# A gated attention/MLP mix on one core: the bias products from GpSimd to VectorE's side work, and a later place for the product with the spread reciprocals

## The chip, the core and the metric

The kernel runs on one core of one Trainium2 chip. The metric is device time in microseconds of one launch. All data are fp32; the large products are made of two or three products of rounded parts (an fp32r part and a remainder), so that each `a @ b` is `ar@br + ar@bl + al@br`.

The engines are named as the profile names them: PE (TensorE, with PEld for its weight loads), DVE (VectorE), ACT (ScalarE), POOL (GpSimd) and SP (SyncE, which here only issues DMAs). POOL issues DMAs as well. Each engine takes its instructions strictly in program order.

## The reference

`x` is 2048 x 512. The output mixes two branches with a gate of each row:

```python
g = sigmoid((x * gate_w).sum(-1, keepdims=True))
q = (x @ wq), 32 heads of 16;  k = x @ wk;  v = x @ wv     # one k and v for all heads
a = softmax(q k^T * 16 ** -0.5) v, heads side by side, @ wo
h = relu(x @ w1 + b1) ** 2                                 # 2048 x 1792
b = h @ w2 + b2
return g * a + (1 - g) * b
```

So `(1 - g) * b2` is one row vector times one number of each row: a 128 x 512 tile of it is one `tensor_scalar` with the broadcast `b2` (`b2t`) and a column of `omg` (1 - g).

## The kernel before

**Attention.** The score matrix is made in units: one unit is 128 keys by 256 queries of four heads. There are 32 groups (4 chunks of 512 rows times 8 groups of four heads) of 32 units each. A unit's scores come out of PE into PSUM (`s`), ACT takes their exponential into `e` (L802), and PE multiplies `e` with the values (`acc`, L825). About two of seven units are relieved: their scores go to a one-bank PSUM tile `x`, DVE copies them to `e` (L786) and ACT takes the exponential there. There is one bank `x`, so a late copy on DVE holds up PE's next score into `x`.

**The rest of the work** is threaded between the scores. PE works on blocks: a block is some units' scores with up to 24 half products ("M") of the other branch between them, then the `acc` products of (mostly) seven units, 56 instructions. What the M's compute comes from a generator of work units: 15 projections of q, then `mlp()`. For each chunk c of 512 rows it yields hidden units (`hidden`, one 128-wide slice f of 1792) in the groups (0..3), (4..7), (8..10), (11..13), and behind each group the four sums of it into `res[c]` (`summed`), which are `res = p * omg + res` on DVE (L700). After chunk c, `res[c]` goes to DRAM (`ress`) by a DMA of POOL (L704); later the output projection reads it back into `big`, adds `g` times its own result and writes `out`. Both of these are POOL DMAs too (L217, L221).

**The bias.** `res[c]` starts as `b2t * omg`: four `tensor_scalar`s of 128 x 512 of POOL at L697, issued when the first group of a chunk is summed. `b2t` is a quarter of a tile called `big`, as is `h[0]`, in which DVE makes the square of relu (L675, L676) before it splits it into `hr` and its remainder (L195, L196). The tile `res` has one buffer (tag `r0`): before the first chunk it belonged to `wqr`, and in each later one it must wait for the DMA of the chunk before.

**The quotients.** When two groups of attention are done, `finish` sends their sums by SP into `oc` (numerators) and `lq` (denominators). `divide` then queues, as DVE work: the bounds and a check of the denominators (L859, L860), the reciprocal `n` (L854) with two POOL DMAs behind it, `ls<-n` (L855) to DRAM and `lc<-ls` (L856) back, which spreads each reciprocal over 16 partitions; and last the product `oc<-oc,lc` (L863), with the DMA `oTs<-oc` of POOL (L897) behind it. There are 15 such quotients.

**What sets the order.** The program's order is made at build time by a planner that keeps a model of the clocks of PE, ACT and DVE. `spend(until)` is called before DVE work that PE waits for and fills DVE's time up to `until` with side work, in this order: remainders of weights that are due, early work (`soon`), `divisions`, `chores` (splitting of loaded tiles into parts). Each entry has a duration and a time from which it may stand; the time of the product `oc<-oc,lc` is the model's end of the copies plus `DIVIDES` (10.0) plus `SPREADS`, so `SPREADS` decides how far behind the reciprocal it stands. None of these figures is a wait on the chip: there every instruction waits for semaphores of what it needs, and those behind it on its engine wait with it.

Of the kernel before, what the change touches and what calls it, by code (L numbers as in the profile page):

```python
# [10 lines left out]
F32 = mybir.dt.float32  # L11
# [4 lines left out]
OP = mybir.AluOpType  # L16
# [16 lines left out]
ROOT = float(0x1fbd1df5 + 0x80000)  # L33
WARM = 10
LW = 4 * CH // 64
LANDS, DIVIDES, WRITES, SPREADS, SURE = 6.0, 10.0, 14.0, 14.0, 1.4
PAIR, CONTEXT, TURN, EXP, COPY, LATE = 0.235, 0.429, 0.36, 0.925, 0.66, 0.3
GROUPS = (0, 1, 2, 3), (4, 5, 6, 7), (8, 9, 10), (11, 12, 13)
AHEAD = 4
# [126 lines left out]
def mix_kernel(ctx: ExitStack, tc: tile.TileContext, xT, wkv, wq, wo, w12, b1, b2, cst, out):  # L166
    nc = tc.nc
# [4 lines left out]
    keep = ctx.enter_context(tc.tile_pool(name="keep", bufs=1))  # L172
# [9 lines left out]
    omg = keep.tile([128, NS], F32, name="omg")  # L182
# [4 lines left out]
    sh = [128, KT, CH]  # L187
# [4 lines left out]
    res = {}  # L192

    def split(r, l, src):
        nc.vector.tensor_copy(r, src)  # L195
        nc.vector.tensor_tensor(l, src, r.bitcast(F32), OP.subtract)  # L196
# [34 lines left out]
    with fast, tc.tile_pool(name="at", bufs=1) as at, \  # L231
# [210 lines left out]
        def stage():  # L442

            if not staged:
                staged.append(keep.tile(sh, F32, name="stage", tag="r2"))
            return staged[0]
# [10 lines left out]
        def dve(d, ready=0.0):  # L457

            nonlocal at_dve
            at_dve = max(at_dve, ready) + d  # L460
            return at_dve
# [30 lines left out]
        def w_rest(half):  # L492
            n = len(ws[half])
            r, l = ws[half][n] = rounded[half][n]
            nc.vector.tensor_tensor(l, wf[half][n], r.bitcast(F32), OP.subtract)
            dve(0.68, since[half][n])
            wanted.append(half)
# [113 lines left out]
        ring, h, b2t, x, osp = [], [], [], dict(enumerate(zip(xr, xl))), {}  # L611

        def later(r, l, src, then=None):

            def cast():
                nc.vector.tensor_copy(r(), src())

            def rest():
                nc.vector.tensor_tensor(l(), src(), r().bitcast(F32), OP.subtract)
                if then:  # L620
                    then()

            chores.extend(((0.46, cast), (0.71, rest)))

        def have(half, n):
            while n not in ws[half]:
                w_split(half)
# [6 lines left out]
        def spend(until=None):  # L634

            nonlocal held

            def fits(d, ready=0.0):
                return until is None or max(at_dve, ready) + d <= until

            while True:
                due = [i for i in halves() if len(rounded[i]) > len(ws[i])]
                if due and fits(0.68, since[due[0]][len(ws[due[0]])]):
                    w_rest(due[0])
                elif soon and fits(soon[0][1]):
                    dve(soon[0][1])
                    soon.pop(0)[2]()
                elif divisions and fits(*divisions[0][:2]):
                    d, ready, f = divisions.pop(0)
                    dve(d, ready)  # L650
                    f()
                elif chores and fits(chores[0][0], held):
                    d, f = chores.pop(0)
                    dve(d, held if d else 0.0)
                    wait = f()
                    if wait:
                        held = max(at_dve, at_pe) + wait
                else:
                    return

        def halves():
            return (0, 1) if len(ws[0]) < begun[0] + 2 else (1, 0)

        def hidden(c, f, hs):

            n = c * NF + f
            have(0, n)
            while c not in x:
                chores.pop(0)[1]()
            (wr, wl), (r, l) = ws[0][n], x[c]  # L670
            begun[0] += 1

            def done(p):
                hr, hl = hs[f] = ring[n % 6]
                nc.vector.tensor_scalar(h[0], p, b1t[:, f:f + 1], 0.0, op0=OP.add, op1=OP.max)  # L675
                nc.vector.tensor_tensor(h[0], h[0], h[0], OP.mult)  # L676
                split(hr, hl, h[0])
                dve(1.9)
                room[0] += 1
                if f == NF - 1 and c < 2:  # L680
                    x_again(c + 2)

            ks = [(k, slice(k * 128, (k + 1) * 128)) for k in range(KT)]
            return ([(wr[:, p], x) for k, p in ks for x in (r[:, k], l[:, k])]
                    + [(wl[:, p], r[:, k]) for k, p in ks], done, None)

        def summed(c, fs, hs):

            n0 = c * NF
            if fs[0] == 0:  # L690
                res[c] = keep.tile(sh, F32, name=f"res{c}", tag="r0")
            have(1, n0 + fs[-1])
            for j in range(4):
                s, cols = 4 * c + j, slice(j * 128, (j + 1) * 128)
                part = res[c][:, j]
                if fs[0] == 0:
                    nc.gpsimd.tensor_scalar(part, b2t[0], omg[:, s:s + 1], None, op0=OP.mult)  # L697

                def done(p, s=s, part=part, j=j):
                    nc.vector.scalar_tensor_tensor(part, p, omg[:, s:s + 1], part, op0=OP.mult, op1=OP.add)  # L700
                    if j == 3:
                        room[1] += len(fs)
                        if fs[-1] == NF - 1:
                            nc.gpsimd.dma_start(ress[c], res[c])  # L704

                yield ([(p[:, cols], ws[1][n0 + f][0]) for f in fs for p in hs[f]]
                       + [(hs[f][0][:, cols], ws[1][n0 + f][1]) for f in fs], done, None)

        def x_again(c):

            r, l = [xp.tile(sh, F32R, name=f"x{n}again{c}", tag=f"x{n}{c - 2}") for n in "rl"]
            def load(a):
                nc.sync.dma_start(stage()[:, :2], xT[c, 2 * a:2 * a + 2].rearrange("k p s -> p k s"))
                return LANDS

            for k in range(KT):
                if k % 2 == 0:
                    chores.append((0.0, lambda k=k: load(k // 2)))
                later(lambda k=k: r[:, k], lambda k=k: l[:, k], lambda k=k: stage()[:, k % 2],
                      (lambda: x.update({c: (r, l)})) if k == KT - 1 else None)  # L720

        def mlp():

            for c in range(NC):
                before, two = None, []
                for fs in GROUPS:
                    hs = {}
                    for f in fs:
                        yield hidden(c, f, hs)
                        o_ready(c)  # L730
                        if c == NC - 1:
                            ask(c, 2)
                        if f == fs[0] and before and fs != GROUPS[-1]:
                            if fs == GROUPS[1] and c > 1:
                                yield from projection(c - 2)
                            yield from summed(*before)
                        elif c > 0 and f > fs[0] and osp.get(c - 1) and c - 1 not in over:
                            yield from projection(c - 1)
                    two = before, (c, fs, hs)
                    before = two[1]  # L740
                for last_two in two:
                    yield from summed(*last_two)
# [227 lines left out]
        def o_ready(c):  # L970

            if c == 0 and not wos:
                wos.extend(xp.tile(sh, F32R, name=n, tag=t) for n, t in (("wor", "xr2"), ("wol", "xl2")))

                def load(a):
                    nc.sync.dma_start(stage()[:, :2], wo[a * 256:a * 256 + 256].rearrange("(t p) n -> p t n", p=128))
                    return WRITES

                for t in range(KT):
                    if t % 2 == 0:  # L980
                        chores.append((0.0, lambda t=t: load(t // 2)))
                    later(lambda t=t: wos[0][:, t], lambda t=t: wos[1][:, t], lambda t=t: stage()[:, t % 2])
            if c > 0:
                ask(c - 1)
# [45 lines left out]
        def projection(c):  # L1030
            if c in over:
                return
            over.add(c)
            yield from wait(c)
            units = list(outproj(c, ots, *osp[c], *wos))
            yield from units[:3]
            terms, done, ahead = units[3]

            def last(p):
                done(p)  # L1040
                used[c] = True

            yield terms, last, ahead
# [258 lines left out]
        for j in range(2, 4):  # L1302
# [3 lines left out]
            s = 4 * (NC - 1) + j  # L1306
# [37 lines left out]
```

## Time and profile before

| what | value |
|---|---|
| median of three runs | 1209.42 us (1207.86 to 1214.25) |
| the profiled execution's own time | 1212.43 us |
| its span, first to last instruction | 1210.7 us |
| mean granted PE clock | 0.995 |
| PE busy | 1190.7 us, 98% of the span |
| ACT busy | 1056.5 us, 87% |
| DVE busy | 744.7 us, 62% |
| POOL busy | 84.4 us, 7% |

A row of the timeline gives start and duration in microseconds, engine, line, operation, output <- input with shapes, and how many instructions were merged (x); in brackets stands the idle time of the engine just before and who ended it. A row of the waits gives the total, the number of times and the longest. A row of the windows gives a stretch, its length, the busy time (and number of instructions) of PE, PEld, DVE, ACT and POOL, then the granted PE clock (1.00 is full), the DMA share and GB/s. A row of the groups ends with the busy time in all and the mean of one in ns, then the idle time before them.

### The profile page before, as it was taken

To read this page: it belongs to the slowest core of one execution; us is meant where nothing else is said; L and a number is where in the kernel's file an instruction comes from. 1 tells how busy PE (TensorE), PEld (TensorE's weight loads), DVE (VectorE), ACT (ScalarE), POOL (GpSimd) and SP (SyncE) were. 2 spreads that over 40 slices of the span, in tenths; PEclk is the share of its full clock that TensorE was granted. 3 is DMA by queue.
4 is the path that set the end of the run, shared out by engine and by line. 5 is a ranking of instruction groups with operands and counts; after the bars stand their busy time and mean duration, and the time that the engine had idled before them with its cause. 6 is when DMAs were issued, how large, how long until landed. Compare 5 with 4: busy or idle time off the path is not lost.

```text
span 1210.7 us, 31619 instructions
## 1 busy us (share of the span) xinstructions
PE 1190.7 (98%) x13685; PEld 789.5 (65%) x13686; DVE 744.7 (62%) x1222; ACT 1056.5 (87%) x1209; POOL 84.4 (7%) x117
## 2 busy tenths in 40 slices
PE   9999899999999999999999999999999999999996
PEld 4566566666666666666666666666666666666663
DVE  6766576666755856657647855657448577556343
ACT  6799799889999889889988988999999899888882
POOL 1001110000000110000002001000001100010000
PEclk9999999999999999999999999999999999999999
DMA  7334432121222222111313123111212222111101
GB/s 230 86 101 116 106 102 64 46 72 55 67 89 93 81 64 97 57 37 44 113 48 115 59 67 106 55 37 54 68 67 64 80 69 92 54 62 40 35 36 38
DMA packets 47656, 89.69 MB, mean 74 GB/s; under 512 B 13642, under 2 KB 14138, under 8 KB 47000
## 3 DMA queue, kind: packets, MB, share of 16 engines
q1 hardware_dynamic: 36664, 64.58, 17.4%
q0 software_dynamic: 10704, 22.77, 5.8%
q8 instruction: 109, 1.79, 0.6%
q14 instruction: 35, 0.29, 0.1%
q10 hardware_dynamic: 144, 0.26, 0.1%
HBM read 61.76 MB, written 21.22 MB: 69 GB/s over the span
## 4 chain that ended last, share of the span: by engine, by line
PE 86%; issue 9%; DVE 2%; DMA 1%; POOL 1%; ACT 0%; SPq 0%; POOLq 0%
PE acc L825 34%; PE mm L1143 29%; PE s L765 17%; PE x L765 4%; POOL qs L358 1%; DMA lc<-ls 1%; DVE e L786 1%; DVE hr L195 0%; DMA xf<-in_xT 0%; PE mm L203 0%; DVE hr L196 0%; PE mm L299 0%; DVE big L676 0%; DVE big L675 0%; PE s L966 0%
## 5 line engine op out<-in xcount | busy, mean ns | idle before, releaser
L802 ACT ACTIVATE e<-s 128x1024 f32<-128x1024 f32 x762 | 748.3, 1029 | 117.4 <-PE s L765 63.7
L786 DVE COPY e<-x 128x512 f32<-128x512 f32 x524 | 361.9, 691 | 406.7 <-PE x L765 334.1
L825 PE MATMUL acc<-e,v_ext 128*32 128x256 f32 (+1 forms) x8064 | 476.2, 385 | 0.0
L765 PE MATMUL s<-qa,k_aug 49*128 49x512 f32 x1524 | 438.2, 416 | 0.1
L825 PEld LDWEIGHTS acc<-e,v_ext 128*32 128x32 f32 x8064 | 247.2, 110 | 198.4 <-issue 55.0
L765 PEld LDWEIGHTS s<-qa,k_aug 49*128 49x128 f32 x1524 | 230.5, 185 | 97.2 <-ACT e L802 73.7
L802 ACT ACTIVATE e<-e 128x1024 f32<-128x1024 f32 x262 | 278.2, 1062 | 3.9 <-DVE e L786 3.9
L765 PE MATMUL x<-qa,k_aug 49*128 49x512 f32 x524 | 218.9, 418 | 9.0 <-DVE e L786 6.8
L1143 PE MATMUL mm<-w2r,hr 64*128 64x512 f32 x752 | 158.2, 394 | 0.0
L765 PEld LDWEIGHTS x<-qa,k_aug 49*128 49x128 f32 x524 | 96.5, 184 | 36.4 <-DVE e L786 13.8
L1143 PEld LDWEIGHTS mm<-w2r,hr 64*128 64x128 f32 x752 | 105.5, 187 | 12.3 <-issue 0.8
L1143 PE MATMUL mm<-w2l,hr 64*128 64x512 f32 x376 | 92.0, 395 | 0.0
L1143 PE MATMUL mm<-xlagain,w1r 64*128 64x512 f32 x224 | 67.3, 392 | 0.0
L1143 PE MATMUL mm<-xragain,w1r 64*128 64x512 f32 x224 | 66.7, 393 | 0.0
L1143 PE MATMUL mm<-xl,w1r 64*128 64x512 f32 x224 | 65.3, 392 | 0.0
L1143 PE MATMUL mm<-xr,w1r 64*128 64x512 f32 x224 | 65.2, 392 | 0.0
L1143 PEld LDWEIGHTS mm<-w2l,hr 64*128 64x128 f32 x376 | 58.9, 188 | 5.8
L1143 PE MATMUL mm<-more 64*128 64x512 f32 x216 | 58.3, 397 | 0.0
L1143 PE MATMUL mm<-xragain,w1l 64*128 64x512 f32 x224 | 51.2, 392 | 0.0
L1143 PE MATMUL mm<-xr,w1l 64*128 64x512 f32 x224 | 50.6, 392 | 0.0
L700 DVE SCALAR_TENSOR_TENSOR res<-mm,omg,res 128x512 f32<-128x512 f32 x64 | 47.5, 741 | 0.0
L855 POOL DMA_DIRECT2D ls<-n x15 | 8.5, 563 | 549.9 <-DVE n L854 494.1
(170 smaller groups left out, 1185.4 us busy)
## 6 DMA issues: line engine op xcount, KB each, us to landing
stage<-in_w SPq DMA_DIRECT2D x56, 256.0 KB
qa<-qs SPq DMA_DIRECT2D x186, 64.0 KB
w1f<-in_w SPq DMA_DIRECT2D x28, 256.0 KB
w2f<-in_w SPq DMA_DIRECT2D x28, 256.0 KB
qs<-qr SPq DMA_DIRECT2D x16, 256.0 KB
ress<-res POOLq DMA_DIRECT2D x4, 1024.0 KB, 4.2
qs<-ql POOLq DMA_DIRECT2D x15, 256.0 KB, 7.7
oc<-accs SPq DMA_DIRECT2D x30, 128.0 KB
```

The lines of the kernel that those rows point to most:

```text
L358: eng.dma_start(bass.AP(tensor=o.tensor, offset=o.offset, ap=[[KS * 2 * CH, 4], [CH, 2 * DH], [1, CH]]), src.bitcast(F32))
L700: nc.vector.scalar_tensor_tensor(part, p, omg[:, s:s + 1], part, op0=OP.mult, op1=OP.add)
L765: nc.tensor.matmul(dst.rearrange("p (a n) -> p a n", a=2), k_aug[rows, kt * 128:(kt + 1) * 128], qa[it][rows, :, q * HC:q * HC + HC], star ...
L786: nc.vector.tensor_copy(e_half(u)[:, 2 * r:2 * r + 2], x.rearrange("p (a n) -> p a n", a=2))
L802: nc.scalar.activation(e_half(u), src, AF.Exp, scale=SCALE)
L825: nc.tensor.matmul(accs[q][h * 32:(h + 1) * 32], v_ext[:, kt], es[u // 2][:, h % 2 * 2 + h // 2, u % 2 * HC:u % 2 * HC + HC * n], start=(k ...
L855: nc.gpsimd.dma_start(ls[i].rearrange("a (b n) -> (a b) n", b=16), n)
L1143: nc.tensor.matmul((self.before if r else self).bank, a[p], b[p], start=not r and i == 0, stop=r == 1 and i == len(self.terms[1]) - 1, ski ...
```

## The change

Two things are changed, and the order on PE stays as it was, row for row.

First, the four bias products of each chunk leave POOL. A list `biases` takes their place: it is filled, and `res[c]` is allocated, once the hidden slice f = 2 of a chunk has been planned, and `spend` takes from it whenever 0.46 us fit, ahead of the chores. They are then `tensor_scalar`s of DVE. If one is still in the list when the first sum needs it, it is issued there.

Second, `SPREADS` goes from 14.0 to 24.0, so that the product `oc<-oc,lc` stands some 10 us further back in DVE's order, and the POOL DMA `oTs<-oc` with it.

```diff
-LANDS, DIVIDES, WRITES, SPREADS, SURE = 6.0, 10.0, 14.0, 14.0, 1.4
+LANDS, DIVIDES, WRITES, SPREADS, SURE = 6.0, 10.0, 14.0, 24.0, 1.4
...
                     d, ready, f = divisions.pop(0)
                     dve(d, ready)
                     f()
+                elif biases and fits(0.46):
+                    bias()
                 elif chores and fits(chores[0][0], held):
...
         def summed(c, fs, hs):
             n0 = c * NF
-            if fs[0] == 0:
-                res[c] = keep.tile(sh, F32, name=f"res{c}", tag="r0")
             have(1, n0 + fs[-1])
             for j in range(4):
                 s, cols = 4 * c + j, slice(j * 128, (j + 1) * 128)
                 part = res[c][:, j]
-                if fs[0] == 0:
-                    nc.gpsimd.tensor_scalar(part, b2t[0], omg[:, s:s + 1], None, op0=OP.mult)
 
                 def done(p, s=s, part=part, j=j):
+                    while (c, j) in biases:
+                        bias()
                     nc.vector.scalar_tensor_tensor(part, p, omg[:, s:s + 1], part, op0=OP.mult, op1=OP.add)
...
+        biases = []
+
+        def bias():
+            c, j = biases.pop(0)
+            s = 4 * c + j
+            dve(0.46)
+            nc.vector.tensor_scalar(res[c][:, j], b2t[0], omg[:, s:s + 1], None, op0=OP.mult)
...
                     for f in fs:
                         yield hidden(c, f, hs)
+                        if f == 2:
+                            res[c] = keep.tile(sh, F32, name=f"res{c}", tag="r0")
+                            biases.extend((c, j) for j in range(4))
                         o_ready(c)
```

**Place 1: DVE while the last projections of q are made** (`qr`, `ql` and `sq` are what DVE makes of one; `e<-x` are the copies of relieved scores). Before, the first product with the spread reciprocals stands two copies behind the split of a projection:

```order
L399 TENSOR_TENSOR sq_143<-qr 128x512
L786 COPY e<-x 128x2x256 x2
L863 TENSOR_TENSOR oc<-oc,lc 128x512
L786 COPY e<-x 128x2x256 x2
L395 CAST qr<-mm 128x512
```

Now (the changed kernel's lines are numbered up to 11 higher):

```order
L399 TENSOR_TENSOR sq_143<-qr 128x512
L797 COPY e<-x 128x2x256 x4
L395 CAST qr<-mm 128x512
L396 TENSOR_TENSOR ql<-mm,qr 128x512
L399 TENSOR_TENSOR sq_143<-qr 128x512
L797 COPY e<-x 128x2x256 x3
L874 TENSOR_TENSOR oc<-oc,lc 128x512
L797 COPY e<-x 128x2x256
L395 CAST qr<-mm 128x512
```

The product has moved past a whole projection and five copies. The other products move in the same way, past some copies each.

**Place 2: DVE behind the split of the second hidden slice of chunk 1** (`orr` and `orl` are the parts of the attention output that the projection will need, `w1l` a remainder of a weight). Before:

```order
L196 TENSOR_TENSOR hr<-big,hr 128x512
L786 COPY e<-x 128x2x256
L619 TENSOR_TENSOR orl<-stage,orr 128x512
L786 COPY e<-x 128x2x256
L495 TENSOR_TENSOR w1l<-w1f,w1r 128x512
L786 COPY e<-x 128x2x256
L616 CAST orr<-stage 128x512
L786 COPY e<-x 128x2x256
L675 TENSOR_SCALAR big<-mm,b1t 128x512
```

Now:

```order
L196 TENSOR_TENSOR hr<-big,hr 128x512
L728 TENSOR_SCALAR res_5002<-big,omg 128x512
L797 COPY e<-x 128x2x256
L495 TENSOR_TENSOR w1l<-w1f,w1r 128x512
L797 COPY e<-x 128x2x256
L728 TENSOR_SCALAR res_5002<-big,omg 128x512
L797 COPY e<-x 128x2x256
L728 TENSOR_SCALAR res_5002<-big,omg 128x512 x2
L797 COPY e<-x 128x2x256
L677 TENSOR_SCALAR big<-mm,b1t 128x512
```

The four bias products take the places of `orl` and `orr`, which move back by one hidden slice, and `w1l` moves ahead by one copy. The other chunks have theirs in the same stretch, chunks 2 and 3 with the fourth behind the next slice.

**Place 3: POOL's queue between two chunks.** Before, the bias products of chunk 1 stand behind the DMA that takes chunk 0 out and between the DMAs of a quotient:

```order
L704 DMA ress<-res_2271 128x2048
L697 TENSOR_SCALAR res_5219<-big,omg 128x512
L855 DMA ls<-n 128x32
L856 DMA lc<-ls 128x1x512
L697 TENSOR_SCALAR res_5219<-big,omg 128x512 x2
L897 DMA oTs<-oc 128x512
L697 TENSOR_SCALAR res_5219<-big,omg 128x512
L217 DMA big<-ress 128x512 x2
```

Now:

```order
L704 DMA ress<-res_2067 128x2048
L866 DMA ls<-n 128x32
L867 DMA lc<-ls 128x1x512
L908 DMA oTs<-oc 128x512
L217 DMA big<-ress 128x512 x2
```

The three rows of bias products are gone, and POOL is left with DMAs alone.

## The prediction

> **What bounds the kernel now.** I read the page's first part, then the timeline of PE for its pace, then the places where that pace breaks, and there DVE and POOL. The first part says which engine has no room:
>
> ```profile
> PE 1190.7 (98%) x13685; PEld 789.5 (65%) x13686; DVE 744.7 (62%) x1222; ACT 1056.5 (87%) x1209; POOL 84.4 (7%) x117
> ```
>
> PE is busy for nearly the whole span, so the change cannot help by making DVE or POOL less busy, only where PE stands still or runs slowly. Since PE's order does not change at all, I compare blocks, from the start of one run of `acc` products to the next. Two ordinary starts, the three around the first break, and what stands on DVE and POOL there:
>
> ```profile
> 172.24 3.23 PE L825 MATMUL acc<-e,v_ext 128*32 128x256 f32 x56
> 180.03 3.23 PE L825 MATMUL acc<-e,v_ext 128*32 128x256 f32 x56
> ...
> 128.48 3.23 PE L825 MATMUL acc<-e,v_ext 128*32 128x256 f32 x56
> 139.84 4.92 PE L825 MATMUL acc<-e,v_ext 128*32 128x256 f32 x56
> 149.29 3.23 PE L825 MATMUL acc<-e,v_ext 128*32 128x256 f32 x56
> ...
> 130.36 0.64 POOL L856 DMA_DIRECT2D lc<-ls  x1 [9.16 <-DMA ls<-n]
> 137.89 0.69 DVE L863 TENSOR_TENSOR oc<-oc,lc 128x512 f32<-128x512 f32 x1 [3.65 <-DMA lc<-ls]
> 139.23 0.49 PE L765 MATMUL x<-qa,k_aug 49*128 49x512 f32 x1 [3.12 <-DVE e L786]
> ```
>
> The pace is 180.03 - 172.24 = 7.79 us. **Break A**: two blocks take 149.29 - 128.48 = 20.81 us. DVE stands 3.65 us at the product with the spread reciprocals, whose DMA was issued at 130.36 and lands at about 137.9; the copy behind it in DVE's queue holds the bank `x`, and PE idles 3.12 us. Then the 56 `acc` products take 4.92 instead of 3.23 us. The windows say why:
>
> ```profile
> 139.80:144.80 5.00, 5.00 (x59) 2.54 (x60) 2.54 (x4) 1.97 (x2) 0.60 (x2) 0.66 0.54 108
> 423.40:427.10 3.70, 3.70 (x18) 2.96 (x20) 2.04 (x4) 1.78 (x2) 0.00 (x0) 0.55 0.00 0
> 172.20:180.00 7.80, 7.80 (x96) 5.26 (x94) 6.88 (x12) 7.00 (x9) 0.53 (x1) 1.00 0.14 31
> ```
>
> Behind A the granted clock is 0.66, in an ordinary block 1.00. The row at 423.40 belongs to **break B**, between chunks 0 and 1; **break C** follows between 1 and 2:
>
> ```profile
> 417.67 1.93 PE L825 MATMUL acc<-e,v_ext 128*32 128x256 f32 x32
> 428.18 3.23 PE L825 MATMUL acc<-e,v_ext 128*32 128x256 f32 x56
> ...
> 706.25 1.93 PE L825 MATMUL acc<-e,v_ext 128*32 128x256 f32 x32
> 712.73 3.23 PE L825 MATMUL acc<-e,v_ext 128*32 128x256 f32 x56
> ...
> 418.80 4.28 POOL L697 TENSOR_SCALAR res<-big,omg 128x512 f32<-128x512 f32 x2
> 419.55 2.11 DVE L195 CAST hr<-big 128x512 fp32r<-128x512 f32 x1
> 423.40 0.53 PE L765 MATMUL x<-qa,k_aug 49*128 49x512 f32 x1 [2.19 <-DVE e L786]
> ...
> 647.44 3.23 PE L825 MATMUL acc<-e,v_ext 128*32 128x256 f32 x56
> 656.75 3.23 PE L825 MATMUL acc<-e,v_ext 128*32 128x256 f32 x56
> ...
> 648.37 6.36 POOL L697 TENSOR_SCALAR res<-big,omg 128x512 f32<-128x512 f32 x4
> 649.65 2.11 DVE L195 CAST hr<-big 128x512 fp32r<-128x512 f32 x1
> 653.51 0.49 PE L765 MATMUL x<-qa,k_aug 49*128 49x512 f32 x1 [1.24 <-DVE e L786]
> ...
> L195 DVE CAST more<-big 128x512 fp32r<-128x512 f32 x9 | 3.8, 427 | 0.3
> ```
>
> The cast of `hr` from `big` takes 2.11 us while POOL's bias products run, against 0.427 us for the same operation elsewhere (last row). The copy behind it is late, PE idles 2.19 us in B and 1.24 in C, and in B the clock falls to 0.55 afterwards. So bias products of an engine that is idle 93% of the time do set PE's end, twice, through DVE.
>
> [...]
>
> **The change part by part.**
>
> *The product, moved back (SPREADS).* A costs 20.81 - 2 x 7.79 = **5.23 us**, 3.6 of standing and 1.7 of slow clock. In place 1 of the order the product now stands five copies and a projection later, just before the copy in the first row below, at about 148.7; less 5.2 us that is 143.5, and the landing at 137.9 does not depend on DVE. So it has 5.6 us to spare, and the gap of 0.67 before that copy takes its 0.69. The 13 other products to which SPREADS applies move by some 10 us too, each with its `oTs` behind it on POOL, which the output projection reads through SP. The other two rows bound that at its tightest, in chunk 3:
>
> ```profile
> 149.40 0.69 DVE L786 COPY e<-x 128x512 f32<-128x512 f32 x1 [0.67 <-PE x L765]
> ...
> 1078.73 0.68 DVE L863 TENSOR_TENSOR oc<-oc,lc 128x512 f32<-128x512 f32 x1
> ...
> 1155.95 0.39 PE L1143 MATMUL mm<-wor,orr 64*128 64x512 f32 x1
> ```
>
> From the product to PE's first use of the parts there are 77 us, of which it takes 10. I take nothing for it, nor for POOL's queue, whose DMAs of this part nobody waits for.
>
> *The bias products off POOL.* B: 10.51 us (428.18 - 417.67) against 6.48 for the block with the same 32 `acc` in front in chunk 2 (712.73 - 706.25): **4.0 us**, 2.2 of standing and 1.8 of slow clock. C: 9.31 - 7.79 = **1.5 us**. The remaining POOL products stretch a DVE instruction here and there without a break in PE's pace: nothing. The gains are 5.2 + 4.0 + 1.5 = 10.7 us.
>
> *The bias products on DVE.* No DVE `tensor_scalar` of 128x512 from SBUF to SBUF stands in the trace. The cast above, also one SBUF tensor in and one out, takes 0.427 us; the same operation with its input in PSUM and a column as scalar takes
>
> ```profile
> L675 DVE TENSOR_SCALAR big<-mm,b1t 128x512 f32<-128x512 f32 x56 | 41.5, 741 | 0.0
> L697 POOL TENSOR_SCALAR res<-big,omg 128x512 f32<-128x512 f32 x16 | 27.4, 1730 | 17.3 <-ACT w1r L500 13.4 <-DMA ress<-res 3.7
> ```
>
> 0.741 us, and POOL needed 1.73. Where the four of a chunk go (place 2), DVE had this room:
>
> ```profile
> 395.66 0.69 DVE L786 COPY e<-x 128x512 f32<-128x512 f32 x1 [0.37 <-PE x L765]
> 396.26 0.68 DVE L619 TENSOR_TENSOR orl<-stage,orr 128x512 fp32r<-128x512 f32 x1
> ...
> 399.06 0.42 DVE L616 CAST orr<-stage 128x512 fp32r<-128x512 f32 x1
> 399.83 0.69 DVE L786 COPY e<-x 128x512 f32<-128x512 f32 x1 [0.35 <-PE x L765]
> ```
>
> That is 0.37 + 0.35 idle, and 0.68 + 0.42 of work that moves back: 1.82 us for 4 x 0.43 = 1.72. The sum fits, the single gaps don't quite: the first product stands in a gap of 0.37, and two stand together. I take 0.1 us a chunk, **0.4** in all. At 0.741 it would be 2.96 - 1.82 = 1.14 a chunk, 4.6 in all, if PE feels each of them; below nothing it cannot go. `orl` and `orr` move back by one slice, a block of 7.8 us; PE reads them only in the projection, a whole group of slices later, and I take nothing for them.
>
> *What DVE now waits for.* POOL used to wait for `b2t` and for `res` to be free, with only DMAs behind it; now DVE would wait, with the copies behind it. For `res` there is time: POOL's product of chunk 1 could start at 382.43, and DVE's first one stands just ahead of the copy at 395.66, 13 us later. For `b2t` there is none to spare:
>
> ```profile
> 141.08 10.17 SPq L358 DMA_DIRECT2D qs<-qr  x2
> ...
> 162.37 0.41 SPq L1059 DMA_DIRECT2D big<-in_b  x1
> ...
> 167.11 0.69 DVE L196 TENSOR_TENSOR hr<-big,hr 128x512 fp32r<-128x512 f32 x1
> ...
> 167.81 4.92 POOL L697 TENSOR_SCALAR res<-big,omg 128x512 f32<-128x512 f32 x3 [13.40 <-ACT w1r L500]
> 168.76 0.42 DVE L616 CAST wor<-stage 128x512 fp32r<-128x512 f32 x1
> ...
> 382.43 1.73 POOL L697 TENSOR_SCALAR res<-big,omg 128x512 f32<-128x512 f32 x1 [3.68 <-DMA ress<-res]
> ```
>
> POOL, idle for 13.4 us, could start at 167.81, just when DVE is done with the split at about 167.75, behind which its first bias product now stands. Both come 5.2 us earlier once A is gone, if SP's chain does: its second `qs<-qr` (the merged row at 141.08 ends at 151.25) is sent when DVE has cast the last `qr`, right behind the copy at 149.40, and from there SP issues on to 162.37. I think that moves along. If `b2` did not come earlier at all, DVE would wait the whole 5.2. Between 0 and 5.2 I take **0.5**, near the row, in which they meet within 0.1.
>
> **The sum**: 10.7 - 0.4 - 0.5 = 9.8 us. Of the profiled execution's 1212.43 us (1.7 of it outside the span) that leaves 1202.6; that execution lies 3.0 above the median of 1209.42, and from the median it is 1199.6. A hangs on when a DMA lands, so part of those 3.0 may be A itself; I take the middle, **1201**.
>
> **The rivals.**
>
> *1. The wait for b2 takes A's place.* For it: the two times meet within 0.1 us, and POOL's DMAs do not all move along and may slow its landing. Against it: SP's issues ahead of 162.37 follow DVE, as said. With the whole 5.2 instead of 0.5, 1205.7.
>
> *2. The product is late again, or the landing moves with it.* The change would not do what it says for A: 1201 + 5.2 = 1206.2. Against it stand 5.6 us to spare.
>
> *3. The long casts do not come from POOL's products.* Then B and C stay, 1201 + 5.5 = 1206.5. For it: the cast at 168.76 took 0.42 in the midst of POOL's products from 167.81. Against it: both casts of 2.11 us lie under such products, and both read `big`, which POOL reads too, while the short one reads `stage`.
>
> *4. Slower: the new product on DVE is as slow as on POOL.* At 1.73 us the four overrun their place by 4 x 1.73 - 1.82 = 5.1 us a chunk, every copy behind them is late by that, and PE waits on the bank `x`: 20.4 in all against 0.4 in the sum, 1201 + 20.0 = 1221. It decides from (10.2 / 4 + 1.82) / 4 = 1.1 us a product. Nothing on DVE of this size and with one input takes that long.
>
> *5. The slow clock is not the stall's doing* and its 1.7 in A and 1.8 in B remain elsewhere: 1204.5. [...] The rows show otherwise: 0.66 and 0.55 right behind 3.12 and 2.19 us of idling, while C, with 1.24, lost only 0.3 beyond that.
>
> **How the numbers follow.** The forecast has 0.72, rival 1 0.09, rivals 2, 3 and 5 0.04 each, rival 4 0.07. The forecast's own range is 1197 (the lowest run, 1207.86, less 10.7) to 1204.5 (the profiled execution less 7.9, with products of 0.741 felt by half). To hold 8 in 10 I take in rivals 1 to 3: 1197 to 1207. A measurement of this kernel can tell about 0.5% from no change, which is 6.0 us: faster means below 1203.4. The forecast lies there in 0.72 x 0.95 = 0.68, the others near 1205 to 1206 in a third of their 0.21: 0.75 in all; the rest of these 0.18; slower, rival 4, 0.07.
>
> **What will show it.** The row of DVE's wait for `lc` is gone and PE has no gap near 134 to 144: part one. No cast of `hr` above 0.5 us, and the blocks that began at 417.67 and 647.44 take about 6.5 and 7.8 us: part two. The 16 new rows of DVE have a mean of 430 ns; above 690 would cost. The first of them, near 162.5, has an idle time in front of it with a DMA as its releaser if rival 1 holds, and PE a gap behind. The prediction is wrong if PE's pace breaks in a new place: first at that one, then at the copies behind the paired bias products.

## The result, and the profile after

The changed kernel takes **1205.87 us** in the median of 20 executions (1200.97 to 1214.08), the kernel before, beside it, 1212.94 (1207.30 to 1220.97). The ratio is 0.9941, 95% interval 0.9922 to 0.9961: faster by 0.4 to 0.8%. The profiled execution took 1207.08 us with a span of 1205.3; that of before had a span of 1210.7. The forecast was 1201, with 1197 to 1207 as its range.

I read the new profile as I read the old one: first the busy times, then PE's pace. The first part of its page:

```profile
PE 1189.2 (99%) x13685; PEld 786.6 (65%) x13686; DVE 745.2 (62%) x1238; ACT 1056.4 (88%) x1209; POOL 56.9 (5%) x101
```

POOL has 16 instructions less and DVE 16 more. DVE's busy time grew by 0.5 us only, though by its groups the products bring 7.3: the casts of `hr` and their remainders take 5.2 us less than before, and the rest is spread over many small differences. The line of the cast, from the views of that line before and after (minimum, median and maximum of one in ns):

```profile
L195 DVE CAST hr<-big x47: 426/427/2114, 158.6 to 1107.9; 128x512 fp32r<-128x512 f32 x47
```

```profile
L195 DVE CAST hr<-big x47: 426/427/429, 153.8 to 1103.5; 128x512 fp32r<-128x512 f32 x47
```

The longest of 47 casts fell from 2.11 to 0.43 us: part two did what it says. Now the timeline of the changed kernel, the starts of PE's blocks around the three old breaks, and DVE's product with the spread reciprocals among them:

```profile
128.73 3.23 PE L836 MATMUL acc<-e,v_ext 128*32 128x256 f32 x56
136.69 3.23 PE L836 MATMUL acc<-e,v_ext 128*32 128x256 f32 x56
143.82 0.68 DVE L874 TENSOR_TENSOR oc<-oc,lc 128x512 f32<-128x512 f32 x1
144.47 3.23 PE L836 MATMUL acc<-e,v_ext 128*32 128x256 f32 x56
...
418.74 1.93 PE L836 MATMUL acc<-e,v_ext 128*32 128x256 f32 x32
425.54 3.23 PE L836 MATMUL acc<-e,v_ext 128*32 128x256 f32 x56
...
644.71 3.23 PE L836 MATMUL acc<-e,v_ext 128*32 128x256 f32 x56
652.49 3.23 PE L836 MATMUL acc<-e,v_ext 128*32 128x256 f32 x56
```

The product has no bracket any more: it waits for nothing. Block against block, before and after:

| place | before, us | after, us | difference |
|---|---|---|---|
| A, two blocks | 20.81 | 15.74 | -5.07 |
| B | 10.51 | 6.80 | -3.71 |
| C | 9.31 | 7.78 | -1.53 |
| the block that begins at 159.56 (164.43 before) | 7.80 | 13.76 | **+5.96** |

The last row is a new break. The timeline of the changed kernel there, with DVE, PE and SP's issue of `b2`:

```profile
159.56 3.23 PE L836 MATMUL acc<-e,v_ext 128*32 128x256 f32 x56
...
162.03 0.42 SPq L1070 DMA_DIRECT2D big<-in_b  x1
162.22 0.69 DVE L196 TENSOR_TENSOR hr<-big,hr 128x512 fp32r<-128x512 f32 x1
...
167.47 0.49 DVE L728 TENSOR_SCALAR res<-big,omg 128x512 f32<-128x512 f32 x1 [4.56 <-DMA big<-in_b]
...
168.61 0.79 PE L776 MATMUL x<-qa,k_aug 49*128 49x512 f32 x1 [4.25 <-DVE e L797]
173.31 3.23 PE L836 MATMUL acc<-e,v_ext 128*32 128x256 f32 x56
```

DVE is through with the split at 162.91 and stands 4.56 us at the first bias product, because `b2` lands at 167.4. The copy behind it frees the bank `x` that much later, and PE idles 4.25 us. The windows of the changed kernel show that its clock suffers afterwards too, while the places of A and B now run at full clock (columns as in the windows of before; the last but two is the granted clock):

```profile
139.80:144.80 5.00, 5.00 (x50) 3.73 (x50) 2.89 (x5) 3.84 (x4) 0.00 (x0) 1.00 0.39 107
...
168.60:173.60 5.00, 4.99 (x34) 3.66 (x38) 3.20 (x7) 1.97 (x2) 0.00 (x0) 0.67 0.15 52
423.40:427.10 3.70, 3.70 (x52) 2.47 (x51) 3.23 (x7) 3.48 (x4) 0.00 (x0) 1.00 0.00 1
```

So of three breaks removed, -10.3 us, this execution gave +6.0 back at a fourth place, 30 us behind the first. That is rival 1.

### The profile page after: what moved, and what is told of

The parts are those of the page before. It is cut to its first block, busy times and chain, and to the rows that moved or that the text cites. A ratio compares the mean times of both kernels' runs of the same rounds, so it can differ in the third digit from the quotient of the medians.

```text
span 1205.3 us, 31610 instructions
## 1 busy us (share of the span) xinstructions
PE 1189.2 (99%) x13685; PEld 786.6 (65%) x13686; DVE 745.2 (62%) x1238; ACT 1056.4 (88%) x1209; POOL 56.9 (5%) x101
## 4 chain that ended last, share of the span: by engine, by line
PE 96%; DVE 2%; DMA 1%; ACT 0%; issue 0%; SPq 0%
PE acc L836 38%; PE mm L1154 32%; PE s L776 19%; PE x L776 5%; DVE e L797 1%; DMA big<-in_b 0%; DMA xf<-in_xT 0%; PE mm L299 0%; PE mm L203 0%; DMA w1f<-in_w 0%; PE s L309 0%; PE s L977 0%; SPq L421 0%; DVE big L678 0%; ACT e L813 0%
## 5 line engine op out<-in xcount | busy, mean ns | idle before, releaser
L677 DVE TENSOR_SCALAR big<-mm,b1t 128x512 f32<-128x512 f32 x56 | 41.6, 743 | 0.0
```

## The experiments

Each kernel was timed beside the kernel before on the same chip; ratios are to that. "After" is the changed kernel.

**1. The later place of the product alone.** The kernel before with one number changed:

```diff
-LANDS, DIVIDES, WRITES, SPREADS, SURE = 6.0, 10.0, 14.0, 14.0, 1.4
+LANDS, DIVIDES, WRITES, SPREADS, SURE = 6.0, 10.0, 14.0, 24.0, 1.4
```

> The kernel before with SPREADS = 24.0 alone; the bias products stay on POOL. Theory (three separate causes): break A near 134 to 149 is gone (20.8 us for two blocks become about 15.7, a gain of 5.1), and DVE waits for no b2, since only POOL does. POOL's products still run, so a cast of hr of 2.1 us with a PE gap of 1.2 to 2.2 us is found again at the two chunk boundaries. What remains of A's gain is cut if ACT, as in the changed kernel, waits 2.2 us for the DMA lq<-accs: by 0 to 2 us. Span about 1206 to 1208, ratio 0.996 to 0.998. Rival (POOL's products have no part in B and C): no cast of hr above 0.5 us at the boundaries, span about 1200 to 1201. Rival (SP's DMAs lag behind whatever DVE does, and the next wait takes all of A back): span about 1210, ratio 1.000.

1206.86 us, ratio 0.9966 (0.9939 to 0.9994). Break A is gone from its trace by the same 5.1 us, and 4.1 of them come back near 160 to 172, where DVE now waits for another late load, with no bias product on it:

```profile
167.46 0.43 DVE L616 CAST wor<-stage 128x512 fp32r<-128x512 f32 x1 [3.25 <-DMA stage<-in_wo]
```

The same kernel has something to say on B and C, because the later products moved POOL's queue. Its timeline, POOL's products and the casts of `hr`:

```profile
418.40 5.82 POOL L697 TENSOR_SCALAR res<-big,omg 128x512 f32<-128x512 f32 x3
419.15 2.11 DVE L195 CAST hr<-big 128x512 fp32r<-128x512 f32 x1
...
423.01 0.50 PE L765 MATMUL x<-qa,k_aug 49*128 49x512 f32 x1 [2.22 <-DVE e L786]
...
647.71 0.43 DVE L195 CAST hr<-big 128x512 fp32r<-128x512 f32 x1
...
659.38 7.28 POOL L697 TENSOR_SCALAR res<-big,omg 128x512 f32<-128x512 f32 x4
```

At C, POOL's four products now start 11.7 us behind the cast, which takes 0.43 us, and the break is gone. At B they stand 0.75 us ahead of it, and it takes 2.11. The long casts go where POOL's products go.

**2. The bias products alone.** After with SPREADS back at 14.0:

```diff
-LANDS, DIVIDES, WRITES, SPREADS, SURE = 6.0, 10.0, 14.0, 24.0, 1.4
+LANDS, DIVIDES, WRITES, SPREADS, SURE = 6.0, 10.0, 14.0, 14.0, 1.4
```

> The changed kernel with SPREADS back at 14.0: the bias products on DVE, the product with the reciprocals where it stood before. Theory (b2 lands at about 167.5 us whether or not A is there): A is back (two blocks take 20 to 21 us), DVE comes to the first bias product at about 167.7 and waits for b2 under 0.5 us, no cast of hr above 0.5 us, B and C are gone: span 1210.7 - 5.3 = about 1205.5, ratio about 0.995. Rival (the wait for b2 comes with the bias products themselves, 4 to 5 us after whatever DVE did before): DVE waits 4 us or more at the first of them, span about 1210 to 1211, ratio about 1.000.

1206.21 us, ratio 0.9966 (0.9939 to 0.9993), but spread from 1200.99 to 1212.64. B and C are gone from its trace. So is break A, although the product stands in its old place:

```profile
128.77 0.64 POOL L867 DMA_DIRECT2D lc<-ls  x1 [7.45 <-DMA ls<-n]
...
134.29 0.68 DVE L874 TENSOR_TENSOR oc<-oc,lc 128x512 f32<-128x512 f32 x1
```

Here the reciprocals were issued at 128.77 and had landed 5.5 us later. In the execution of before they were issued at 130.36 and took 7.5. A is therefore not a fixed property of the order: it depends on how long two transfers take in an execution.

The new break is there in small. SP issues `b2` 1.73 us earlier than in after, DVE is through with the split as early as there (162.81, in after 162.91), and it waits for `b2` all the same, neither under 0.5 us as the theory said nor 4 us or more as the rival did:

```profile
160.30 0.40 SPq L1070 DMA_DIRECT2D big<-in_b  x1
...
164.38 0.48 DVE L728 TENSOR_SCALAR res<-big,omg 128x512 f32<-128x512 f32 x1 [1.56 <-DMA big<-in_b]
```

PE idles 1.25 us behind it, and the block takes 9.30 us in place of 13.76.

**3. The first bias product one hidden slice later**, to let `b2` land:

```diff
-                        if f == 2:
+                        if f == (3 if c == 0 else 2):
```

> The changed kernel, with the bias products of chunk 0 put into the list one hidden slice later (f = 3 instead of 2), so that the first one stands a block, 7.8 us, further back; nothing else is changed. Theory (the 13.76 us block is DVE's wait for b2): no wait of DVE for big<-in_b, the block takes 7.8 us, and 1205.3 - 6.0 = about 1199.3 of span; if ACT's wait of 2.2 us for lq<-accs at 163 then holds PE up by itself, up to 2 us of it come back: 1199 to 1201.5, ratio 0.989 to 0.992. Rival (b2 was only the first of several late transfers, the next wait takes its place): the block near 160 still takes 11 us or more, span 1203 to 1205.

1204.11 us, ratio 0.9949 (0.9927 to 0.9971). The first bias product stands at 172.02 and waits for nothing. The load issued just ahead of `b2` is the next to be late: the cast of `wor` from `stage`, which experiment 1 also waited for.

```profile
165.94 0.43 DVE L616 CAST wor<-stage 128x512 fp32r<-128x512 f32 x1 [1.68 <-DMA stage<-in_wo]
```

The block takes 9.00 us, 1.2 too many, in place of 13.76.

**4. `b2` loaded by ACT**, past SP's queue and at the same place of the program:

```diff
-                    nc.sync.dma_start(b2t[0], bass.AP(tensor=b2.tensor, offset=b2.offset, ap=[[0, 128], [1, D]]))
+                    nc.scalar.dma_start(b2t[0], bass.AP(tensor=b2.tensor, offset=b2.offset, ap=[[0, 128], [1, D]]))
```

> The changed kernel, with the DMA of b2 issued by ACT's queue instead of SP's, where it stands behind SP's reads of q and its writes of the norms; nothing else is changed. Theory (b2 is late because SP issued it at 162.03 behind its other transfers, not because the transfer is slow): it is issued some 5 to 10 us earlier, DVE waits for it under 1 us, span 1199 to 1201.5 as with a later first product, plus under 0.5 us for ACT's issue. Rival (the DMA engines are what is late): it is issued earlier but lands after 165 all the same, DVE still waits 2 us or more, span 1203 to 1205.

1202.30 us (1200.91 to 1204.54), ratio 0.9931 (0.9904 to 0.9959). Its timeline at that place, ACT's issue and DVE's first bias product:

```profile
155.60 0.38 ACTq L1070 DMA_DIRECT2D big<-in_b  x1
156.03 0.63 ACT L500 ACTIVATE w1r<-stage 128x512 fp32r<-128x512 f32 x1 [1.60 <-DMA qa<-qs]
...
163.44 0.48 DVE L728 TENSOR_SCALAR res<-big,omg 128x512 f32<-128x512 f32 x1
```

`b2` is issued 6.4 us earlier than in after, and no wait is left on DVE. ACT, which waits there for a load of `qa`, stands 1.60 us; the block around it takes 7.82 us, 0.46 more than before. Between 2 and 1161 us PE has no gap above 0.6 us.

**5. Second traces of both kernels**, unchanged, to see what is the program's and what an execution's.

> The kernel before, unchanged, for a second trace. If break A hangs on when one DMA of the spread reciprocals lands, and that varies from run to run, its wait of 3.65 us is shorter or absent in some traces, while breaks B and C (POOL's products beside DVE's casts, both fixed by the program) are there each time, B with 3 to 4 us and C with 1.5. If A is fixed by the program too, it is there again with 5.2 us in two blocks.

> The changed kernel, unchanged, for a second trace. If the wait for b2 hangs on when DMAs ahead of it land, DVE's wait in front of the first bias product is another than 4.56 us here (between 0 and 5), and the block behind it is longer than 7.8 us by that wait's excess over about 0.3 us of spare time plus the slow clock. If it is fixed by the program, it is 4.3 to 4.8 us again and the block takes 13 to 14 us.

They took 1214.41 and 1206.82 us, with spans of 1212.6 and 1205.1. In both, PE stood in neither of the two places that depend on a landing. The timeline of before, second trace, at A, then of after, second trace, at the new break:

```profile
134.54 0.64 POOL L856 DMA_DIRECT2D lc<-ls  x1 [7.01 <-DMA ls<-n]
...
140.66 0.69 DVE L863 TENSOR_TENSOR oc<-oc,lc 128x512 f32<-128x512 f32 x1
```

```profile
163.31 0.41 SPq L1070 DMA_DIRECT2D big<-in_b  x1
...
168.65 0.48 DVE L728 TENSOR_SCALAR res<-big,omg 128x512 f32<-128x512 f32 x1
```

They were about as long as the first traces all the same, because both started late. The windows of before, second trace and first:

```profile
26.00:41.00 15.00, 14.94 (x67) 11.63 (x68) 9.56 (x20) 8.75 (x10) 0.00 (x0) 0.54 0.25 85
```

```profile
26.00:41.00 15.00, 14.94 (x118) 9.92 (x118) 13.23 (x27) 11.26 (x13) 0.90 (x1) 1.00 0.28 85
```

In the second trace of before the granted clock is 0.54 from 26 to 41 us (in that of after 0.50 from 30 to 40), with PE busy throughout: 67 instructions in place of 118. PE is about 6 us late from there on (its block of 128.48 begins at 134.81). POOL's and SP's transfers do not run late by as much (`b2` was issued at 163.31 against 162.03), so what they bring has landed when DVE asks for it. In these traces an execution pays for either the late start or the waits at A and for `b2`, never for both. B and C are there in both traces of before: B with 10.51 and 10.40 us, C with 9.31 and 9.31.

**6. Products on POOL that nobody uses**, to test the cause of B and C by itself. Experiment 4's kernel with the 16 products put back on POOL where they stood, the result to a tile that is free at that time; the bias stays on VectorE.

```diff
                 part = res[c][:, j]
+                if fs[0] == 0:
+                    nc.gpsimd.tensor_scalar(ots[0], b2t[0], omg[:, s:s + 1], None, op0=OP.mult)
```

> The version with b2 loaded by ACT, in which POOL does no bias products, and in it 16 products on POOL again, where they stood before the change, from the same b2 to a tile that nobody reads at that time. They take part in nothing, and the bias itself stays on VectorE. Theory (breaks B and C come from POOL's products, through DVE's casts): casts of hr of about 2.1 us are back under POOL's products near the starts of chunks 1 and 2, PE has a gap of 1 to 2.2 us behind each, the blocks near 415 and 640 us take 8 to 10 us instead of 6.9 and 7.8, and the time is 2 to 5 us above the version without them (1202.3): 1204 to 1207. Rival (the long casts have another cause, such as SP's or POOL's DMAs or the waits for res): casts of hr stay at 0.43 us, and the time at 1201 to 1203.

1204.45 us, ratio 0.995 (0.9934 to 0.9966). The median is above that of experiment 4, though the intervals meet; what the trace shows is weaker than the theory: the cast near B takes 0.84 us, PE idles 0.83 and the block takes 7.60 us; C shows nothing, since POOL's products start 13 us behind the cast.

The same with `k_aug[:, :D].bitcast(F32)` in place of `b2t[0]`:

> The same 16 idle products on POOL, but they read another tile (the keys, as fp32) instead of the tile `big`, in which hr's source also lies. Theory A (two engines at work at once in the same tile of SBUF, `big`, disturb each other): casts of hr back at about 0.43 us, DVE instructions at most some tenths longer under POOL's products, the time at 1201 to 1203. Theory B (any POOL product and any DVE cast or copy from SBUF to SBUF that meet in time disturb each other, wherever the data lies): casts of about 2.1 us as in the run with `big` as source, the time the same as there within 2 us.

1203.99 us, ratio 0.9953 (0.9938 to 0.9969): no difference. Its timeline near B:

```profile
416.59 1.40 DVE L196 TENSOR_TENSOR hr<-big,hr 128x512 fp32r<-128x512 f32 x1
416.74 5.44 POOL L697 TENSOR_SCALAR big<-k_aug,omg 128x512 f32<-128x512 f32 x3
```

So POOL's products need not read `big` to slow DVE: the second half of DVE's split, 0.69 us elsewhere, takes 1.40 beside products that read the keys, and a cast of `orr` at 418.51 takes 0.86, where the next one, at 421.30, takes 0.42. A cast of 2.1 us occurs from 412 to 432 us in neither of the two runs, so for that length the question stays open.

With SPREADS at 14.0 in the kernel of the first of these, POOL's queue has its old order:

> As the run with idle products that read b2, but with SPREADS back at 14.0, which gives POOL's queue the order that it has before the change (product, ls, lc, two products, oTs, product in chunk 1). Theory (how much a POOL product costs DVE depends on where it falls among DVE's casts, not on what it is for): POOL's two products start 0.5 to 1 us ahead of the first cast of hr of chunk 1, that cast takes 2.1 us, PE's gap is 1.5 to 2.3 us and the block takes 9 to 10.5 us instead of 6.9; in chunk 2 a cast of 2.1 us and a block of 9.3; the time is 4 to 5.5 us above the changed kernel with b2 by ACT (about 1206). Rival (the casts were long because the sums in res, which POOL wrote, were waited for): casts of at most 0.9 us, blocks of at most 7.7, and 1202 to 1204.

1206.09 us, ratio 0.9954 (0.993 to 0.9979). At B the products start 0.39 us behind the cast (0.83 us). At C they stand as before the change, 1.28 us ahead of the cast, and yet:

```profile
647.54 6.87 POOL L697 TENSOR_SCALAR big<-big,omg 128x512 f32<-128x512 f32 x4
...
648.82 0.58 DVE L195 CAST hr<-big 128x512 fp32r<-128x512 f32 x1
```

0.58 us, not 2.11: against the theory. What differs is that the four idle products write one tile, so each waits for the one before, and they take 6.87 us in place of 6.36. Break A is back in this trace, by the way, with the product's old place: DVE waits 3.75 us for `lc`.

The last of this kind writes two tiles in turn (`ots[j % 2]`), so that the second product can follow the first at once:

> As the idle products in their old place, except that they write two tiles in turn. There each of POOL's products waited for the one before it, since all four wrote the same tile; here the second starts as soon as the first is out of the way, as before the change. In the earlier run the cast of hr of chunk 2 stood 1.28 us behind the start of POOL's four products, exactly as before the change, and took 0.58 us, not 2.11. Theory (products back to back keep DVE out through the second one; a wait between them lets it in): in chunk 2 the cast of hr takes 1.8 to 2.2 us again if it starts 1.0 to 1.5 us behind the first product, PE has a gap of about 1.2 us and the block takes 9.2 to 9.4 us. Rival (what the products write, or the tile res, made the casts long): the cast stays below 0.9 us and the block at 7.8.

```profile
642.06 6.36 POOL L697 TENSOR_SCALAR big<-big,omg 128x512 f32<-128x512 f32 x4
...
643.34 2.12 DVE L195 CAST hr<-big 128x512 fp32r<-128x512 f32 x1
...
647.20 0.50 PE L778 MATMUL x<-qa,k_aug 49*128 49x512 f32 x1 [1.25 <-DVE e L799]
```

With the same 1.28 us between them the cast takes 2.12 us, PE idles 1.25 and the block takes 9.30 us: break C as it was (2.11, 1.24, 9.31), made by products whose results nobody uses. By its ratio, 0.9994 (0.9966 to 1.0023), this kernel has nothing left of the gain; C is only 1.5 us of that, A can be back in executions with the product's old place, and what else went was not pursued.

**7. Experiment 4's kernel and after on the same chip.**

> The changed kernel with b2 loaded by ACT, once more, beside the changed kernel itself on the same chip. Theory (of the changed kernel's executions, those without a slow start wait for b2 or for other late loads, and this version removes that wait): its median lies 2 to 5 us below the changed kernel's, its lowest time within 0.7 us of the changed kernel's lowest, since that one had no wait. Rival (the wait was one execution's accident): the two medians are the same within 1 us.

> The changed kernel beside the one with b2 by ACT. Theory: a median of 1204 to 1207, 2 to 5 us above the other, with executions near 1201 that have no wait and executions near 1206 that wait for b2 or start slowly. Rival: the median within 1 us of the other's.

`b2` by ACT: 1201.84 us (1201.05 to 1207.36), ratio 0.9929 (0.9902 to 0.9956). After: 1203.04 (1200.73 to 1209.24), ratio 0.9935 (0.9912 to 0.9959). The medians lie 1.2 us apart, between the two expectations, and the intervals overlap: in the median no difference is shown. After's trace has the new break once more, longer than the first time:

```profile
161.90 0.41 SPq L1070 DMA_DIRECT2D big<-in_b  x1
...
168.54 0.48 DVE L728 TENSOR_SCALAR res<-big,omg 128x512 f32<-128x512 f32 x1 [5.20 <-DMA big<-in_b]
```

PE idles 4.88 us behind it, the block takes 15.51, and the span is 1207.5; that of the other kernel, without a wait, 1200.0. Of all timed executions of after, 10 of 27 stay below 1203 us; of `b2` by ACT, 12 of 14. The lowest are alike, 1200.73 and 1200.91. That fits a wait that some executions of after have and this version has not.

## Why the prediction was right, and where it failed

**A.** In the execution that I had a trace of, the step was right in kind and size: 5.23 us forecast, 5.07 gone, standing and slow clock together. What I took for the program's is one execution's: of five traces with the product in its old place two have the wait (3.65 us before, 3.75 with the idle products in their old place) and three have not (experiment 2, before again, idle products back to back). The gain of this part is thus about 5 us in an execution that has the wait and nothing in one that has not. I did see that A hangs on a landing, and used it only to move the sum by half of 3.0 us.

**B and C.** Forecast 4.0 and 1.5, measured 3.71 and 1.53. For B I had taken the block of chunk 2 (6.48 us) as the ordinary one; that of chunk 3 takes 6.83 before the change, and B takes 6.80 now. The mechanism, POOL's products beside DVE's casts, is shown by experiments 1, 2 and 6: long casts leave with the products, follow them to other places and, at C, come back in full with products that do nothing. At B the idle products never stood 0.75 us ahead of the cast as they do in before; from 0.06 to 0.39 us behind its start they made casts of 1.04 to 0.83 us, so B's full size was not made again. Of rival 3's arguments one was false: that the casts read `big`, as POOL does, is not the reason, since products that read the keys stretch DVE's instructions as well. Why the cast at 168.76 stayed short in the midst of POOL's products I did not settle.

**The slow clock behind B**, 1.8 us of the 4.0, was there in both traces of before (0.55 from 423.4 to 427.1 us in the first, 0.73 from 424.5 to 428.0 in the second), but did not come every time: in experiment 1 PE idled 2.22 us there and kept the full clock (1.00 from 423.0 to 426.7). Its block took 8.99 us, not 10.5. Rival 5 is out for A and B of the first trace, since the clock there is 1.00 once the stalls are gone.

**The products on DVE.** One takes 0.48 us, not 0.43 (the line's view, minimum, median and maximum in ns):

```profile
L728 DVE TENSOR_SCALAR res<-big,omg x16: 476/480/486, 167.5 to 924.2; 128x512 f32<-128x512 f32 x16
```

The 0.4 us that I took for them do not show. In place 2, the two blocks in which the four stand (from 393.04 and 400.82) take 7.79 and 7.80 us, against 7.79 and 7.82 before. So four products of 0.48, 1.92 us, fit where I had counted 1.82 us of room. Rival 4 is out.

**The wait for b2 is the step that failed.** I wrote that "both come 5.2 us earlier once A is gone, if SP's chain does", that "I think that moves along", and took 0.5 us. DVE came 4.84 us earlier (the split ends at 162.91, before at about 167.75), `b2`'s issue 0.34 us earlier. The price was 5.96 us, 4.25 of standing and the rest slow clock, above even the 5.2 of rival 1, in which I had counted no slow clock. SP's rows show where its lead went, after and then before:

```profile
146.53 9.06 SPq L435 DMA_DIRECT2D qa<-qs  x8
155.69 0.54 SPq L902 DMA_DIRECT2D oc<-accs  x1
157.38 0.57 SPq L903 DMA_DIRECT2D lq<-accs  x1
```

```profile
151.35 6.42 SPq L435 DMA_DIRECT2D qa<-qs  x8
157.86 0.54 SPq L891 DMA_DIRECT2D oc<-accs  x1
158.45 0.57 SPq L892 DMA_DIRECT2D lq<-accs  x1
```

The first of these steps did move along: the loads of `qa` begin 4.82 us earlier. But the eight of them take 9.06 us in place of 6.42, and the lead is down to 2.17 at `oc`, 1.07 at `lq` and 0.34 at `b2` (162.03 above, 162.37 before). SP does not only follow DVE; it also waits for transfers, and these were issued sooner here but took longer. The list of who waited for whom in after names one such wait:

```profile
SPq L903 <- DMA qa<-qs: 1.1, 1, 1.1
```

I had followed the chain from `b2` back to the last wait for DVE, and had not asked what else stood between. The same lag of the transfers fits experiments 1 and 3: whoever asks first in this stretch waits, be it for `b2` or for `in_wo`.

A second step may have failed with it. For the product's later place I took nothing "for POOL's queue, whose DMAs of this part nobody waits for". But that place also moved the write behind the product, from 139.82 before to

```profile
146.72 0.59 POOL L908 DMA_DIRECT2D oTs<-oc  x1
```

right behind POOL's write of `ql` at 146.02. That write lands 10.9 us after its issue, the one that stood alone at 146.69 before after 6.7. Experiment 2, with `oTs` in its old place (137.63) and DVE as early as in after, tells the two parts of the loss from each other: SP's lead is 2.07 us at `oc` there, as in after, but still 2.07 at `b2`, where after has 0.34, and the wait is 1.56 us instead of 4.56. So the larger part of the lead is lost without the moved write, and the rest only with it. These are single traces, and what sets the pace of the transfers was not tested: that the moved write costs that rest is not shown.

**The total.** That 1205.87 lies in the range is in part luck. It is outside the forecast's own 1197 to 1204.5, and inside only because the range took in rivals 1 to 3; rival 1 is the one that came in the profiled execution. The two wrong sizes do not cancel: A counted nearly whole, which three of five traces do not have, and the wait for `b2` counted almost not at all both made the forecast too low. Of the 4.9 us between 1201 and 1205.87, 3.5 lie in the kernel before, which took 1212.94 in this measurement and 1209.42 in the three runs that I started from; the gain, 7.1 us, is 1.4 short of the 8.4 forecast. That rival 1's 1205.7 lies so near is accident for the same reason. Through the profiled pair the account closes to 0.2: -5.07 - 3.71 - 1.53 + 5.96 = -4.35 at the four places, of -5.4 between the spans; 0.2 lie in the block that began at 924 us, and about 1.0 in the last 45 us, whose cause I did not trace.

## What to carry to other kernels

Before a stall's whole length is booked as gain, go on along the path for a few stages and ask of each load there whether it was issued by the clock of the engine that comes sooner, or by the landing of other transfers: what waits for transfers may stay where it was, and become the next stall, as here, where DVE came 4.84 us earlier and the issue of `b2` 0.34. Ask, too, what a moved instruction takes along: a DMA behind it moves with it, here from 139.82 to 146.72 us, right behind another write. An idle engine is not a free one; here two of POOL's instructions back to back held up a cast of DVE for longer (2.12 us) than with a wait between them (0.58). And a stall that hangs on a landing is worth a second trace, because it may be one execution's: the one at A stood in two of five traces.

## What the hardware showed that I had not expected

- **Back to back counts.** With POOL's products one behind the other a DVE cast took 2.12 us; with a semaphore wait between the first two it took 0.58, at the same distance of 1.28 us. The cast of 2.12 us, from 643.34 to 645.46, outlasts the first product (642.06 + 6.36 / 4 = 643.65) by more than its own 0.43, and ends near the end of the second (642.06 + 6.36 / 2 = 645.24), so the second one seems to have come ahead of it. The ends of the products in the other two cases, taken one by one in before and estimated in the other, bear this out: C's cast before the change ends at 651.77, 0.29 us behind the second product (651.48), and the short one of 0.58 at 649.40, near the end of the first (647.54 + 6.87 / 4 = 649.26). B is another case: there the cast ends at 421.66, long before the second product does (423.08), and why it takes 2.11 us stays open. By what means a product holds a cast up, no run shows.
- **The clock fell without a stall, and in pieces.** From 26 to 41 us it was granted at 0.54 in the second trace of before, though PE was busy 14.94 of these 15.00 us. And a stall of 2.2 us cost clock in two traces (0.55 behind 2.19 us in the first of before, 0.73 behind 2.27 in the second) but none in another (1.00 behind 2.22, in the window below, of experiment 1). Windows cut to fit show what these shares are made of: the clock is 0.50 from 140.43 to 143.84 and from 423.74 to 427.15 in before and from 168.44 to 171.85 in after, 3.41 us each, and 1.00 on both sides; in the late start of before's second trace it is 0.50 for four times as long (26.76 to 40.40, estimated from its windows of 2 us: 0.69 from 26 to 28, 0.90 from 40 to 42, 0.50 in those between). In these three places one piece costs 3.41 / 2 = 1.7 us of full speed, whether the stall was of 2.19, 3.12 or 4.25 us: that is about the 1.7, 1.8 and 1.7 us of slow clock counted in A, B and the new break. Why a piece came behind a stall of 2.19 us, none behind one of 2.22, and four without a stall, no run shows.

```profile
423.00:426.70 3.70, 3.69 (x34) 2.69 (x38) 2.87 (x5) 2.38 (x3) 1.23 (x1) 1.00 0.00 0
```
